# A mixer kernel's opening: chunk-wise transposes, tile-wise normalisation and the order of the first maxima

## The chip, the cores and the metric

The kernel runs on one core of a Trainium2 chip. The metric is the device time of one execution in microseconds (us), taken as the median of several runs. The engines are named as the profile names them: PE multiplies matrices (PEld loads its weights), DVE is the vector engine, ACT the scalar engine with its function tables, POOL the general engine, and SP issues the DMAs. Each engine works through its own queue in order and waits on semaphores for the others. PSUM is the memory that PE writes to; it has eight banks of 128 x 512 floats, and this kernel uses all of them.

## The reference

`x` is 2048 tokens by 512 features. It is normalised, goes through windowed attention with 32 heads of 16 features, and the result is gated by a small MLP of a second normalisation:

```python
xn = _layernorm(x)                                   # no gain, no bias
q, k, v = split(xn @ wqkv)                           # 32 heads, 16 features each
scores = q . k * 16**-0.5, kept where 0 <= query - key < 256
s = softmax(scores) @ v  -> (2048, 512) @ wo
y = _layernorm(xn)
g = silu(gelu(y @ w1 + b1) @ w2 + b2)                # 512 -> 1792 -> 512
out = x + s * g
```

Everything is float32. The kernel keeps that precision by splitting an operand into a high half and a low half (the rest that the high half leaves) and adding three products: high by high, high by low, low by high.

## The kernel before

Tokens are worked in four chunks of 512, each of four tiles of 128 tokens. For a chunk the kernel loads four tiles `xs[c]`, normalises them, transposes them on PE into banks `tr` (sixteen 128 x 128 transposes, one bank for each 128 features `kt`), and `split` writes the transposed chunk as a high half (cast on ACT) and a low half (subtraction on DVE) into `big`, called xnT in the profile. A layer norm of one tile is `bn_stats` and `bn_aggr` on DVE, an addition of eps on DVE, a power of -1/2 on POOL (`rs`), a shift on DVE and the application, an activation on ACT with scale and bias. `layernorm` has two forms. The grouped one makes the statistics of all four tiles and then one power and one shift for the four; the eager one finishes tile by tile. Before the change chunk 0 (`ln`) is eager, and chunks 1 to 3 (`ln1`, `ln2`, `ln3`) are grouped.

Heads are worked in eight groups of four. For a group n, `job_qk` multiplies a chunk with the group's q and k weights (twelve products of 128 x 512, profile name fb), and its `finish` splits the result and sends it in DMAs (`qk<-sh` for the high half, `qk<-pjr` for the low half) into the rows of a slot, from which scores are multiplied. `job_v` makes v for two blocks of 128 keys (24 products of 128 x 256, name pv) and copies them into `vt` on ACT. A slot's other rows have to hold constants: `clear_rows` writes them, ahead of the rows that the DMAs set.

Softmax needs a maximum for each query ahead of the exponentials. `max_block(n, qb)` multiplies the scores of one block of 128 queries into xy (two banks) and zo (half of two banks), merges them under a mask on DVE and reduces them on DVE, 12 blocks ahead (`LEAD`) of `prob_block`, which multiplies the scores again (stb), takes the exponential on ACT and cuts the window's edges on POOL. `pv_step` multiplies the probabilities with v into `otb`, a part of zo, and copies it out; each fourth copy is sent to `oT_d` by a DMA. `max_rows` turns four blocks' maxima into rows and sends them into the slot.

The order is written out by hand. A main loop runs over steps t from -16 to 128. Step t holds `max_block` for block t + 12, the lists `fills[t, 0]` and `fills[t, 1]` (products spread over the steps), `plan[t]` (`at`), `prob_block`, `pv_step`, `lns[t]` (layer norm steps) and `ends[t]` (`behind`). Steps -16 to -1 have no probabilities: they make projections 0 and v for all four chunks and the first twelve maxima. `groups` gives chunk c the four steps from 4c - 16, with its projection, v, the transposes of chunk c + 1, and v again. Every engine keeps this order (`Ordered`, whose line L43 all instructions carry in the profile, so that the profile is read by tile names); SP kept it only from the loop on, and the scheduler ordered its DMAs ahead of that. Ahead of the loop stands a prologue: loads, constants, chunk 0's layer norm, transposes and weight splits.

PSUM is shared out as xy (two banks), zo (two), fb0 and fb1 (one each, taken in turns by `fill_bank`) and two banks of the pool `ps_st`, which the transposes' first two banks and the v products take in turns until step 0. There the pool closes and stb takes its place.

Of the kernel before, what the change touches and what calls it, by code (L numbers as in the profile page):

```python
# [9 lines left out]
F32 = mybir.dt.float32  # L10
# [15 lines left out]
NEG = -3.0e38  # L26
LEAD = 12
EARLY = 10
FW = 128


class Ordered:
# [18 lines left out]
def mixer_kernel(ctx, tc, x, wqk, wv, wo, w1, b1, w2, b2, out):  # L51
# [27 lines left out]
        nc.sync.dma_start(t, src)  # L79
        return t  # L80

    def layernorm(ts, name, on_act, eager=False):


        n = len(ts)
        mv = small.tile([P, n, 2], F32, tag="mv", name=f"mv{name}")
        rs = small.tile([P, n], F32, tag="rs", name=f"rs{name}")
        sh = small.tile([P, n], F32, tag="shift", name=f"shift{name}")

        def each(i):  # L90

            stats(i)
            ve = small.tile([P, 1], F32, tag="ve1", name=f"ve{name}_{i}")
            nc.vector.tensor_scalar(ve, mv[:, i, 1:2], EPS, None, op0=ALU.add)
            nc.gpsimd.tensor_tensor(rs[:, i: i + 1], ve, mhalf[:, :1], op=ALU.pow)

        def shift(i):
            nc.vector.scalar_tensor_tensor(sh[:, i: i + 1], mv[:, i, 0:1], -1.0, rs[:, i: i + 1],
                                           op0=ALU.mult, op1=ALU.mult)

        def stats(i):
            st = small.tile([P, 6], F32, tag="bn", name=f"bn{name}_{i}")
# [12 lines left out]
        def apply(i):  # L115
            if on_act:
                nc.scalar.activation(ts[i], ts[i], AF.Identity, bias=sh[:, i: i + 1], scale=rs[:, i: i + 1])
            else:
                nc.vector.tensor_scalar(ts[i], ts[i], mv[:, i, 0:1], rs[:, i: i + 1],
                                        op0=ALU.subtract, op1=ALU.mult)  # L120
        if eager:
            return [(lambda i=i: each(i), lambda i=i: shift(i), lambda i=i: apply(i)) for i in range(n)]
        return [lambda i=i: stats(i) for i in range(n)] + [invert, shift_all] + [lambda i=i: apply(i) for i in range(n)]

    def run(steps):
# [43 lines left out]

    vt = vp.tile([P, NKB, 16, DH + 1], F32, name="vt")  # L170

    def clear_rows(i):

        for qk in range(2):
            nc.sync.dma_start(slots[i][3:P:4, qk].rearrange("r p (k t) -> r (p k) t", t=FW).bitcast(F32),
                              fill[:, qk].unsqueeze(1).to_broadcast([32, 4096 // FW, FW]))

    ident = const.tile([P, P], F32, name="ident")
    upper = const.tile([P, P], F32, name="upper")
    mhalf = const.tile([P, 4], F32, name="mhalf")  # L180
    negc = const.tile([P, 1], F32, name="negc")
    nc.vector.memset(negc, NEG)
    nc.vector.memset(otb, 0.0)
    mask = upper.bitcast(I32).unsqueeze(1).unsqueeze(1).to_broadcast([P, 2, 2, P])
# [60 lines left out]
    def job_qk(n, c):  # L245

        box = []
        ops = [(kt, a, b) for kt in range(KT) for a, b in PASSES]
        if not n and not c:
            ops.sort(key=lambda o: o[2])  # L250
        sl = slice(512 * c, 512 * (c + 1))

# [10 lines left out]
        def finish():  # L263
            hi = sgp.tile([P, 512], F32R, tag="sh", name=f"sh_{n}_{c}", bufs=2)
            raw = t2.tile([P, 512], F32, tag="t2", name=f"pjr_{n}_{c}")
            lo = raw.bitcast(F32R)
            nc.scalar.copy(raw, box[0])

            def high():
                nc.scalar.copy(hi, raw)  # L270
                behind(now[0], send_high)

            def send_high():
                for qk, tt in ((1, 0), (0, 0), (1, 2), (0, 1)):
                    send(hi, qk, tt)

            def low():
                (nc.gpsimd if n else nc.vector).tensor_tensor(lo, raw, hi.bitcast(F32), op=ALU.subtract)
# [205 lines left out]
    def pv_step(n, qb, also=()):  # L484
# [118 lines left out]
    for i in range(4):  # L603
        nc.sync.dma_start(xs[2][i], x[1024 + P * i: 1024 + P * (i + 1), :])
    nc.gpsimd.memset(mhalf, -0.5)
    make_identity(nc, ident)
    fill = const.tile([32, 2, FW], F32, name="fill")
    for qk in range(2):
        nc.gpsimd.memset(fill[:, qk], float(qk))
    ln = layernorm(xs[0], "A0", True, True)  # L610
# [12 lines left out]
    n, raw = raws["qk"]  # L623
    nc.gpsimd.tensor_tensor(wqs[0][:, 1], raw, wqs[0][:, 0].bitcast(F32), op=ALU.subtract)
    for j, raw in enumerate(raws["v"]):
        nc.gpsimd.tensor_tensor(wva[:, 1, 2 * j: 2 * j + 2], raw, wva[:, 0, 2 * j: 2 * j + 2].bitcast(F32),
                                op=ALU.subtract)
    nc.gpsimd.memset(vt[:, :, :, DH: DH + 1], 1.0)
    nc.gpsimd.memset(upper, 1.0)
# [7 lines left out]
    for i in range(4):  # L637
        nc.sync.dma_start(xs[3][i], x[1536 + P * i: 1536 + P * (i + 1), :])
    for i in range(4):
        nc.sync.dma_start(xn_d[i], xs[0][i])  # L640
    for i in range(4):
        at(-15, nc.sync.dma_start, xn_d[4 + i], xs[1][i])
# [75 lines left out]
    fills[16 * NQ, 0] = [(first_h, (0,))]  # L718
    at(16 * NQ, activate_first)

    ln3 = layernorm(xs[3], "A3", True)
    lns = {-16: ln1[8:] + ln2[5:6], -14: ln2[6:8], -13: ln2[8:] + ln3[0:5], -12: ln3[5:8], -11: ln3[8:]}
    def fill_in(t, half):
        now[:] = t, half
        run(delayed.pop((t, half), ()))
# [1 line left out]
            fn(*args)  # L727

    end = 16 * NQ
    nc.sync.on = True  # L730
    for t in range(-16, end + 1):
        m = t + LEAD
        if t == -5:
            open_slot(1)
            clear_rows(1)
        if 0 <= t < end:
            if t == 0:
                early.close()
                stb.append(attn.enter_context(tc.tile_pool(name="ps_s2", bufs=1, space=PSUM)).tile(
                    [P, 2, 512], F32, name="stb"))  # L740
            prob_block(t // 16, t % 16, 1)
        if 0 <= m < end:
# [12 lines left out]
        for fn, args in ends.get(t, []):  # L755
            fn(*args)
    for k in sorted(delayed):
        run(delayed[k])
    for fn, args in plan[end + 1]:
        fn(*args)  # L760
    nc.sync.on = False
    first_h(1)
# [193 lines left out]
```

## Time and profile before

| | us |
|---|---|
| median of 3 runs | 789.29 (787.99 to 789.78) |
| the profiled execution | 788.93 |
| its span in the profile | 787.2 |
| PE busy | 752.4 |
| DVE busy | 483.9 |
| ACT busy | 372.4 |
| POOL busy | 311.7 |
| first product of step 0 (stb) starts at | 73.81 |
| first PE instruction of the program starts at | 6.48 |

The profile shows one execution. A line of the timeline gives the start from the span's first instruction, the time that the group took, the engine, the line, the operation, what it wrote and read, its shape and how many there were; brackets at its end give the idle time of the engine before it, and what ended that. The page's 40 slices are 19.7 us each, with a digit for each slice in tenths of busy time.

### The profile page before, as it was taken

To read this page: it belongs to the slowest core of one execution; us is meant where nothing else is said; L and a number is where in the kernel's file an instruction comes from. 1 tells how busy PE (TensorE), PEld (TensorE's weight loads), DVE (VectorE), ACT (ScalarE), POOL (GpSimd) and SP (SyncE) were. 2 spreads that over 40 slices of the span, in tenths; PEclk is the share of its full clock that TensorE was granted. 3 is DMA by queue.
4 is the path that set the end of the run, shared out by engine and by line. 5 is a ranking of instruction groups with operands and counts; after the bars stand their busy time and mean duration, and the time that the engine had idled before them with its cause. 6 is when DMAs were issued, how large, how long until landed. Compare 5 with 4: busy or idle time off the path is not lost.

```text
span 787.2 us, 18487 instructions
## 1 busy us (share of the span) xinstructions
PE 752.4 (96%) x7420; PEld 584.8 (74%) x7420; DVE 483.9 (61%) x751; ACT 372.4 (47%) x626; POOL 311.7 (40%) x586
## 2 busy tenths in 40 slices
PE   5799999999999999999999999999999999999997
PEld 4687666666768887666666677788888888888886
DVE  5686777777777678878883558733355235532243
ACT  4643766767676666777877734321113111221111
POOL 4101665757565554767766744310112010110101
PEclk9999999999999999999999999999999999999999
DMA  8633445645446763555624282520123011210011
GB/s 272 217 75 85 109 111 130 157 109 139 110 92 213 231 217 94 131 151 138 190 88 151 81 300 82 189 87 13 54 81 116 5 41 40 82 55 13 27 54 67
DMA packets 55061, 90.46 MB, mean 115 GB/s; under 512 B 10496, under 2 KB 14848, under 8 KB 54976
## 3 DMA queue, kind: packets, MB, share of 16 engines
q1 hardware_dynamic: 54976, 89.29, 39.4%
q8 instruction: 58, 0.95, 0.5%
q14 instruction: 27, 0.22, 0.1%
HBM read 44.05 MB, written 25.95 MB: 89 GB/s over the span
## 4 chain that ended last, share of the span: by engine, by line
PE 80%; DVE 8%; ACT 5%; issue 3%; DMA 2%; POOL 1%; SPq 0%; DVEq 0%; ACTq 0%; POOLq 0%
PE acc L43 17%; PE fb L43 16%; PE h L43 15%; PE zo L43 12%; PE stb L43 7%; PE s L43 6%; PE xy L43 5%; ACT pt L43 3%; DVE xy L43 2%; DVE mt L43 2%; PE pv L43 2%; DVE xnT L43 1%; POOL pt L43 1%; PE yt L43 1%; DVE gl L43 1%
## 5 line engine op out<-in xcount | busy, mean ns | idle before, releaser
L43 POOL TENSOR_SCALAR_AFFINE_SELECT pt<-pt 128x256 f32<-128x256 f32 x480 | 195.2, 431 | 176.6 <-ACT pt L43 175.2
L43 ACT ACTIVATE pt<-stb 128x768 f32<-128x768 f32 (+1 forms) x244 | 188.6, 773 | 58.1 <-PE stb L43 48.4
L43 DVE TENSOR_REDUCE mt<-xy 128x4 f32<-128x1024 f32 (+1 forms) x128 | 152.6, 1192 | 4.4
L43 PE MATMUL acc<-w,gh 128*128 128x512 f32 x432 | 133.5, 390 | 0.3 <-DVE gh L43 0.2
L43 DVE COPY_PREDICATED xy<-upper,zo 128x512 f32<-128x512 int32 x112 | 77.6, 693 | 71.8 <-PE zo L43 69.8
L43 ACT ACTIVATE g<-h,b1s 128x512 f32<-128x512 f32 x44 | 30.3, 688 | 190.0 <-PE h L43 190.0
L43 PE MATMUL fb<-xnT,wqb 64*128 64x512 f32 (+1 forms) x696 | 117.7, 404 | 0.8 <-DVE xnT L43 0.6
L43 DVE CAST gh<-g 128x512 fp32r<-128x512 f32 x52 | 28.4, 546 | 137.6 <-PE acc L43 124.8
L43 PE MATMUL zo<-pt,vt 128*17 128x128 f32 x2880 | 103.7, 275 | 2.5 <-DVE xy L43 1.9
L43 PE MATMUL stb<-qk 64*128 64x384 f32 (+1 forms) x488 | 96.6, 392 | 7.5 <-ACT pt L43 6.0
L43 PEld LDWEIGHTS zo<-pt,vt 128*17 128x17 f32 x2880 | 67.6, 97 | 39.6 <-issue 17.9
L43 PEld LDWEIGHTS acc<-w,gh 128*128 128x128 f32 x432 | 80.8, 188 | 18.0 <-DVE gh L43 1.5
L43 PE MATMUL h<-xnT 128*128 128x512 f32 x320 | 92.0, 389 | 0.0
L43 PE MATMUL acc<-w,gl 128*128 128x512 f32 x216 | 84.6, 392 | 1.3 <-DVE gl L43 1.2
L43 PEld LDWEIGHTS stb<-qk 64*128 64x128 f32 x488 | 45.6, 183 | 52.2 <-ACT pt L43 41.2
L43 PEld LDWEIGHTS fb<-xnT,wqb 64*128 64x128 f32 (+1 forms) x696 | 65.5, 186 | 8.2 <-DVE xnT L43 0.9
L43 PEld LDWEIGHTS h<-xnT 128*128 128x128 f32 x320 | 60.1, 188 | 12.5
L43 PE MATMUL xy<-qk 64*128 64x256 f32 (+2 forms) x536 | 61.3, 302 | 4.9 <-DVE mt L43 2.3
L43 PE MATMUL h<-yh,xnT 128*128 128x512 f32 x160 | 55.7, 389 | 0.0
L43 PEld LDWEIGHTS xy<-qk 64*128 64x128 f32 x536 | 44.1, 185 | 15.6 <-DVE mt L43 6.5
L43 ACT COPY oraw<-zo 128x128 f32<-128x128 f32 x128 | 34.1, 267 | 38.3 <-PE zo L43 33.8
L43 POOL TENSOR_TENSOR or<-or,w 128x512 f32<-128x512 f32 x16 | 20.7, 1296 | 74.9 <-DMA or<-oT_d 65.6
(115 smaller groups left out, 959.9 us busy)
## 6 DMA issues: line engine op xcount, KB each, us to landing
qk<-sh SPq DMA_DIRECT2D x128, 128.0 KB
qk<-pjr SPq DMA_DIRECT2D x64, 128.0 KB
oT_d<-oraw SPq DMA_DIRECT2D x32, 256.0 KB
w_d<-in_w_dram SPq DMA_DIRECT2D x14, 512.0 KB
x<-in_x_dram SPq DMA_DIRECT2D x16, 256.0 KB
or<-oT_d SPq DMA_DIRECT2D x16, 256.0 KB
w<-rden_d SPq DMA_DIRECT2D x16, 256.0 KB
xo<-in_x_dram SPq DMA_DIRECT2D x16, 256.0 KB
```

The costliest lines, as they stand in the source:

```text
L43: r = issue(*args, **kwargs)
```

## The change

It has six parts, five of them ahead of step 0.

1. Chunk 0 is transposed tile by tile into four banks that are open at once (two of `ps_st` and the two halves of xy): as soon as a token tile is applied, its four transposes are issued. Tile 3 is applied on DVE, the others on ACT. The high halves of wv are cast on DVE, not on ACT.
2. Chunks 1 to 3 are normalised eagerly, tile by tile, and tiles 2 and 3 of chunk 1 are applied on DVE. Chunks 2 and 3 go in pairs of tiles, at the ends of steps -15, -13, -12 and -11. Before, the statistics of chunk 1 and most of chunk 2 stood in the prologue, and the rest in steps -16 to -11. Chunk 1's transposes go to both halves of xy, to zo and to one bank of `ps_st`, and half of a v product stands ahead of them.
3. `clear_rows` fills the whole slot by memsets and a copy on DVE, ACT and POOL (slot 0) or on POOL alone (slot 1); before, DMAs wrote the rows that need a constant.
4. PE gets products of constants: sixteen at the start, and three after each of the first three tiles' transposes.
5. In steps -12 to -1 `max_block` stands behind products: behind both halves of `fills` for blocks 0 to 3 and between them for blocks 4 to 11. Before, it stood ahead of them. Group 0's projections are split straight from PSUM, without the copy to SBUF, and chunk 1's projection is ordered as chunk 0's was (high halves of x first).
6. The DMA to `oT_d` is issued at the end of its step, not in the middle. SP keeps the written order from the loads of chunk 2 on, and the eight DMAs that save the normalised tiles (`xn_d`) go at the ends of steps -14 and -13.

```diff
-    def layernorm(ts, name, on_act, eager=False):
+    def layernorm(ts, name, on_act, eager=False, n_act=4):
...
-        def apply(i):
+        def apply(i, on_act=on_act):
             if on_act:
                 nc.scalar.activation(ts[i], ts[i], AF.Identity, bias=sh[:, i: i + 1], scale=rs[:, i: i + 1])
...
+        def end(i):
+
+            if i < n_act:
+                shift(i)
+            apply(i, i < n_act)
         if eager:
-            return [(lambda i=i: each(i), lambda i=i: shift(i), lambda i=i: apply(i)) for i in range(n)]
+            return [(lambda i=i: each(i), lambda i=i: end(i)) for i in range(n)]
...
-    def clear_rows(i):
-
-        for qk in range(2):
-            nc.sync.dma_start(slots[i][3:P:4, qk].rearrange("r p (k t) -> r (p k) t", t=FW).bitcast(F32),
-                              fill[:, qk].unsqueeze(1).to_broadcast([32, 4096 // FW, FW]))
+    def clear_rows(i, parts):
+
+        flat = slots[i].rearrange("p q l t -> p (q l t)")
+        ones = upper.unsqueeze(1)
+        for eng, lo, hi in parts:
+            if eng is nc.scalar:
+                eng.copy(flat[:, lo: hi].rearrange("p (k t) -> p k t", t=P), ones.to_broadcast([P, (hi - lo) // P, P]))
+            else:
+                eng.memset(flat[:, lo: hi].bitcast(F32), float(lo >= 4096))
...
+    nc.vector.memset(upper, 1.0)
+    for _ in range(16):
+        nc.tensor.matmul(fb[0][:, 0:P], upper, upper, start=True, stop=True)
+    nc.gpsimd.memset(mhalf, -0.5)
+    make_identity(nc, ident)
+    clear_rows(0, ((nc.vector, 0, 2048), (nc.scalar, 4096, 7168), (nc.gpsimd, 2048, 4096), (nc.gpsimd, 7168, 8192)))
...
             if i == 0:
-                box.append(ps_st.tile([P, 512], F32, tag="b", name=f"tr_{c}_{kt}") if kt < 2 else fill_bank())
+                box.append(xy[:, kt] if c == 1 and kt < 2 else zo[:, 0] if c == 1 and kt == 2 else
+                           ps_st.tile([P, 512], F32, tag="b", name=f"tr_{c}_{kt}") if kt < 2 or c == 1 else fill_bank())
...
-        if not n and not c:
+        if not n and c < 2:
             ops.sort(key=lambda o: o[2])
...
-            nc.scalar.copy(raw, box[0])
+            src = raw if n else box[0]
+            if n:
+                nc.scalar.copy(raw, box[0])
...
-            at(16 * n + qb + 2, nc.sync.dma_start, oT_d[n // 2, n % 2::2, :, P * (qb - 3): P * (qb + 1)], outs[0])
+            behind(16 * n + qb + 2, nc.sync.dma_start, oT_d[n // 2, n % 2::2, :, P * (qb - 3): P * (qb + 1)], outs[0])
...
+    tr0 = [ps_st.tile([P, 512], F32, tag="b", name=f"tr_0_{kt}") for kt in range(2)] + [xy[:, 0], xy[:, 1]]
+
+    def transpose0(i):
+        for kt in range(KT):
+            nc.tensor.transpose(tr0[kt][:, P * i: P * (i + 1)], xs[0][i][:, P * kt: P * (kt + 1)], ident)
+        for _ in range(3 if i < 3 else 0):
+            nc.tensor.matmul(fb[0][:, 0:P], ident, ident, start=True, stop=True)
+
+    ln = layernorm(xs[0], "A0", True, True, 3)
     for i in range(4):
         ln[i][0]()
         if i:
             ln[i - 1][1]()
-            ln[i - 1][2]()
-        if i == 3:
-            split_wqk(0)
+            transpose0(i - 1)
     ln[3][1]()
-    ln[3][2]()
-    for _, mm, k in job_x(0)[0]:
-        mm(k)
-    split_wv(0)
+    transpose0(3)
+    split_wqk(0)
     n, raw = raws["qk"]
     nc.gpsimd.tensor_tensor(wqs[0][:, 1], raw, wqs[0][:, 0].bitcast(F32), op=ALU.subtract)
     for j, raw in enumerate(raws["v"]):
+        nc.vector.tensor_copy(wva[:, 0, 2 * j: 2 * j + 2], raw)
         nc.gpsimd.tensor_tensor(wva[:, 1, 2 * j: 2 * j + 2], raw, wva[:, 0, 2 * j: 2 * j + 2].bitcast(F32),
                                 op=ALU.subtract)
+    for kt in range(KT):
+        split(big[:, 0, kt, 0:512], big[:, 1, kt, 0:512], tr0[kt])
+    ln1 = layernorm(xs[1], "A1", True, True, 2)
+    for i in range(4):
+        ln1[i][0]()
+        if 0 < i < 3:
+            ln1[i - 1][1]()
...
-    clear_rows(0)
-    ln1 = layernorm(xs[1], "A1", True)
-    run(ln1[0:4])
-    ln2 = layernorm(xs[2], "A2", True)
-    run([ln1[4], ln2[0], ln1[5], ln2[1], *ln1[6:8], ln2[2], ln2[3], ln2[4]])
...
+    for i in range(8):
+        behind(-14 + i // 4, nc.sync.dma_start, xn_d[i], xs[i // 4][i % 4])
 
     def group(c):
+        if c == 0:
+            (ops, finish), (x_ops, _) = job_v(0, 1), job_x(1)
+            return [job_qk(0, 0), job_v(0, 0), (ops[:12] + x_ops, lambda: None), (ops[12:], finish)]
...
-    ln3 = layernorm(xs[3], "A3", True)
-    lns = {-16: ln1[8:] + ln2[5:6], -14: ln2[6:8], -13: ln2[8:] + ln3[0:5], -12: ln3[5:8], -11: ln3[8:]}
+    def pair(l, a):
+        return [l[a][0], l[a + 1][0], l[a][1], l[a + 1][1]]
+
+    ln2, ln3 = (layernorm(xs[c], f"A{c}", True, True) for c in (2, 3))
+    lns = {-16: [ln1[2][1], ln1[3][1]], -15: pair(ln2, 0), -13: pair(ln2, 2), -12: pair(ln3, 0), -11: pair(ln3, 2)}
...
-            clear_rows(1)
+            clear_rows(1, ((nc.gpsimd, 0, 4096), (nc.gpsimd, 4096, 8192)))
...
-        if 0 <= m < end:
+        if t >= 0 and m < end:
             max_block(m // 16, m % 16)
         fill_in(t, 0)
         for fn, args in plan.get(t, []):
             fn(*args)
+        if 4 <= m < LEAD:
+            max_block(0, m)
         if 0 <= t < end:
             prob_block(t // 16, t % 16, 0)
         fill_in(t, 1)
+        if 0 <= m < 4:
+            max_block(0, m)
```

More of the change, by code (lines that the diff above doesn't have):

```diff
@@ L28 @@
 EARLY = 10
-FW = 128
 class Ordered:
@@ L266, in finish @@
             lo = raw.bitcast(F32R)
-            nc.scalar.copy(raw, box[0])
+            src = raw if n else box[0]
+            if n:
+                nc.scalar.copy(raw, box[0])
             def high():
-                nc.scalar.copy(hi, raw)
+                nc.scalar.copy(hi, src)
                 behind(now[0], send_high)
@@ L277, in low @@
             def low():
-                (nc.gpsimd if n else nc.vector).tensor_tensor(lo, raw, hi.bitcast(F32), op=ALU.subtract)
+                (nc.gpsimd if n else nc.vector).tensor_tensor(lo, src, hi.bitcast(F32), op=ALU.subtract)
                 behind(now[0], send_low)
@@ L602, in mixer_kernel @@
         xs[c] = [x23[:, 4 * (c - 2) + i] for i in range(4)]
[L603 to L610, printed above, removed]
+    nc.sync.on = True
+    for c in (2, 3):
+        for i in range(4):
+            nc.sync.dma_start(xs[c][i], x[512 * c + P * i: 512 * c + P * (i + 1), :])
+    tr0 = [ps_st.tile([P, 512], F32, tag="b", name=f"tr_0_{kt}") for kt in range(2)] + [xy[:, 0], xy[:, 1]]
[5 more added lines that the diff above has]
+    ln = layernorm(xs[0], "A0", True, True, 3)
     for i in range(4):
@@ L625, in mixer_kernel @@
     for j, raw in enumerate(raws["v"]):
+        nc.vector.tensor_copy(wva[:, 0, 2 * j: 2 * j + 2], raw)
         nc.gpsimd.tensor_tensor(wva[:, 1, 2 * j: 2 * j + 2], raw, wva[:, 0, 2 * j: 2 * j + 2].bitcast(F32),
                                 op=ALU.subtract)
+    for kt in range(KT):
+        split(big[:, 0, kt, 0:512], big[:, 1, kt, 0:512], tr0[kt])
+    ln1 = layernorm(xs[1], "A1", True, True, 2)
+    for i in range(4):
+        ln1[i][0]()
+        if 0 < i < 3:
+            ln1[i - 1][1]()
     nc.gpsimd.memset(vt[:, :, :, DH: DH + 1], 1.0)
-    nc.gpsimd.memset(upper, 1.0)
     nc.gpsimd.affine_select(out=upper, in_=upper, pattern=[[1, P]], compare_op=ALU.is_gt,
                             fill=0.0, base=0, channel_multiplier=-1)
-    clear_rows(0)
-    ln1 = layernorm(xs[1], "A1", True)
-    run(ln1[0:4])
-    ln2 = layernorm(xs[2], "A2", True)
-    run([ln1[4], ln2[0], ln1[5], ln2[1], *ln1[6:8], ln2[2], ln2[3], ln2[4]])
[L637 to L642, printed above, removed]
+    for i in range(8):
+        behind(-14 + i // 4, nc.sync.dma_start, xn_d[i], xs[i // 4][i % 4])
     def group(c):
+        if c == 0:
+            (ops, finish), (x_ops, _) = job_v(0, 1), job_x(1)
+            return [job_qk(0, 0), job_v(0, 0), (ops[:12] + x_ops, lambda: None), (ops[12:], finish)]
         return [job_qk(0, c), job_v(0, 2 * c), *([job_x(c + 1)] if c + 1 < NCH else []), job_v(0, 2 * c + 1)]
@@ L729, in mixer_kernel @@
     end = 16 * NQ
-    nc.sync.on = True
     for t in range(-16, end + 1):
@@ L758, in mixer_kernel @@
         run(delayed[k])
-    for fn, args in plan[end + 1]:
+    for fn, args in ends[end + 1]:
         fn(*args)
```

## The prediction

> **What bounds the kernel now.** I read the page first (busy shares, the 40 slices), then the chain, then windows and the timeline of the first 85 us, because every edit but one stands there.
>
> ```profile
> PE 752.4 (96%) x7420; PEld 584.8 (74%) x7420; DVE 483.9 (61%) x751; ACT 372.4 (47%) x626; POOL 311.7 (40%) x586
> PE   5799999999999999999999999999999999999997
> PE 80%; DVE 8%; ACT 5%; issue 3%; DMA 2%; POOL 1%; SPq 0%; DVEq 0%; ACTq 0%; POOLq 0%
> ```
>
> PE is the bound nearly everywhere; only the first two slices (39 us) show it waiting. The order on every engine behind step t = 0 is the same before and after, except for one DMA per four steps, so what the change makes of the time is how much earlier or later step 0 comes. Its first product starts at 73.81 us in the profile, and behind it the lag carries to the end.
>
> ```profile
> 20.00:25.00 5.00, 2.41 (x9) 1.56 (x10) 2.97 (x10) 4.55 (x8) 1.02 (x1) 0.84 0.95 341
> 30.00:35.00 5.00, 3.56 (x20) 2.78 (x20) 3.03 (x8) 1.97 (x4) 1.01 (x1) 1.00 0.25 69
> 35.00:40.00 5.00, 5.00 (x47) 4.66 (x46) 3.60 (x5) 4.13 (x7) 0.00 (x0) 1.00 0.49 111
> 40.00:45.00 5.00, 4.56 (x40) 4.02 (x38) 4.97 (x7) 3.04 (x7) 0.00 (x0) 1.00 0.21 46
> ```
>
> The columns after the stretch are PE, weight loads, DVE, ACT and POOL busy. Summed by windows PE idles 12.5 us up to 30 and 3.0 us from there to 75: all that can be won is before 32 us. From 40 to 45 DVE is already full (4.97 of 5).
>
> **What the edits cost.** All LayerNorm chunks now go tile by tile, as chunk 0 does already:
>
> ```profile
> 7.10 0.69 DVE L43 BATCH_NORM_STATS2 bnA<-x 128x6 f32<-128x512 f32 x1
> 8.11 0.15 DVE L43 SCALAR_TENSOR_TENSOR shiftA<-mvA,rsA 128x1 f32<-128x1 f32 x1
> 8.27 0.55 POOL L43 TENSOR_TENSOR rsA<-veA,mhalf 128x1 f32<-128x1 f32 x1 [0.53 <-DVE shiftA L43]
> 28.13 0.69 DVE L43 BATCH_NORM_STATS2 bnA<-x 128x6 f32<-128x512 f32 x1
> 28.95 0.66 DVE L43 BATCH_NORM_STATS2 bnA<-x 128x6 f32<-128x512 f32 x1
> 11.51 1.84 PE L43 MATMUL fb<-ident,x 128*128 128x128 f32 x8
> 39.76 1.04 PE L43 MATMUL fb<-ident,x 128*128 128x128 f32 x8
> ```
>
> From 7.10 one tile takes DVE 1.08 us with its small operations; in the grouped form 0.82 (28.13 to 28.95). DVE also stands still for POOL's power (0.56) ahead of the last shift. A transpose costs 0.24 us at the low clock, 0.13 at the full one.
>
> *Chunk 0.* x3 is applied on DVE at 8.86 (behind the power, 8.27 + 0.55) instead of on ACT at 9.52. The row y<-y gives 0.54, so it is done at 9.40 against 10.33, and four transposes follow, not thirteen. The constant products stand ahead of them. The trace has no plain f32 product of 128 columns; its bounds are the transpose (0.13 to 0.24) and the 128x512 product (3.03 for 12, 0.25). I take 0.25, since PE gets its first work at 1.1: then three products and four transposes take 1.27 a tile, and the first bank is complete at about 11 (9.95 to 15). DVE meanwhile makes both high halves of wv, moved to it from ACT, while POOL subtracts. What that does shows late in the trace:
>
> ```profile
> 468.31 0.43 DVE L43 CAST gh<-g 128x512 fp32r<-128x512 f32 x1 [5.54 <-PE acc L43]
> 473.75 1.55 DVE L43 CAST gh<-g 128x512 fp32r<-128x512 f32 x1 [0.16 <-PE acc L43]
> 473.71 2.74 POOL L43 TENSOR_TENSOR wos<-wos 128x512 fp32r<-128x512 f32 x2
> ```
>
> The same cast takes 0.43 alone and 1.55 beside POOL's subtraction. So the copies end at 11.4 (0.43 + 1.55 from 9.4), not 10.3. Then come the four splits: casts of 0.58, subtractions of 0.69. In the built order the fourth cast waits for the third subtraction, because both read the one tile xy. That gives 11.75, 12.4, 13.1, 13.8, a cast to 14.4 and the last subtraction to 15.1. Before, it ended at 14.69: nothing is won (bounds 13.9, copies and products free, and 18.5, products at the low clock).
>
> *Chunk 1.* Four tiles at 1.08 from 15.1, power, and the apply on DVE (0.54): x3 of the chunk is ready at 20.55 (before 23.5). PE does fb and both v products meanwhile and transposes the first bank by 20.9. The second bank is xy's other half, and in the built order its first transpose waits for the DVE subtraction of the first half. That waits for its ACT cast, and this stands behind the applies of two x2 tiles. Two halves of one tile do wait for each other in this kernel, as the view of waits shows; otb is a part of zo that the masked copy does not touch:
>
> ```profile
> PE zo L43 <- DVE xy L43: 1.9, 6, 0.5
> ```
>
> DVE: pjr 0.69 to 21.25, two x2 tiles to 23.4, power and shift to 24.1; ACT: apply 0.81 to 24.95, cast to 25.55; DVE: subtraction to 26.3. PE stands 5.4 us. Then twelve transposes at 0.24 (29.2), the second half of v (1.9, 31.1), fb 2.99 (34.1) and the first maxima product 0.44: 34.55. Before, the same work ended at 34.79. Again nothing.
>
> The transposes are priced at 0.24 because the trace shows what such a gap does: behind the idle time from 20 to 23 us the granted clock is 0.50 from 24 to 26 and 1.00 from 27.
>
> *Chunk 2.* Before, DVE had all of x2's and x3's statistics done by 31.4. Now it has two x2 tiles and four x3 tiles left, between the maxima. DVE in its order: x2 tiles to 33.55; maxima 0 (0.75 + 0.69, from 34.6) to 36.05; two x3 tiles with power 38.95; pjr 39.65; maxima 1 (0.76 + 1.23) 41.65; two x3 tiles 44.55. ACT must apply both (0.81 each, to 45.5) before its first cast of chunk 2 (46.1), and DVE's subtraction ends at 46.8. PE: v 37.65, maxima 38.0, first bank 38.5; the next bank waits for the copy of vt, which stands on ACT behind two x3 applies (40.55); transposes 42.1, maxima 42.7. The next v product waits for a bank until 46.8, and runs to 49.95; maxima 3 waits for DVE (three subtractions, 0.69 + 1.23) to 50.75 and ends at 51.35. Before, that work was done at 44.72: 6.6 us late. This is the term that decides: idle 2.05 + 4.15 + 0.8. If the gap of 4.15 halves the clock as that at 20 to 23 did, for some 3 us, v costs 1.5 more, of which 0.8 hides in the wait for maxima 3: +0.7, kept for the range.
>
> The Trainium skill (TensorE: Matmul & The Clock Gate, Part 1) says that the clock halves after an idle window of about 3.4 us and returns after as long a busy one. By that rule the v product would start slow and the sum would be some 0.9 higher; the trace has one such spell, and agrees.
>
> *Chunk 3 to step 0.* DVE's backlog is gone. PE waits 0.55 for maxima 3, then runs as before; the small waits before (0.52 at 59.4) are partly hidden by putting maxima behind products. My sum reaches the end of maxima 9 and fb at 70.1, against 63.79: 6.3 late. Step 0 is at 80.1.
>
> *The rest.* Projection 0 is split straight from PSUM: an ACT copy of 0.56 less for each chunk, and the bank is held until DVE's subtraction (39.65), ahead of the transposes that want it. The four DMAs that set the rows go; their cover was idle queue time. On SP they and eight xn_d writes no longer stand ahead of the first rows, which land by about 26 (needed at 34.1): the 1.7 us that PE waited for them at 31.4 is in the sum. Engines set slot 0 instead: 2048 on DVE before x lands at 3.41, 3072 on ACT (0.81 for 768, so under 3.3 us) before 5.6, and 3072 on POOL. POOL's rows bound that: ident (0.204 for 128, 0.098 for one, 0.83 ns an element) ends it at 4.2 and costs nothing, vt (0.576 for 256, 1.87 ns) at 7.2 and then delays the first power of 4.59, +1.9. I take ident, a plain fill like this. Slot 1 takes POOL twice 3.4 us from 61.7, free until step 0. The output DMA moved behind the step passes three or four row DMAs on SP (0.55 each); PE's only row wait there is 0.7: 0 to -0.7, I take 0.
>
> **Sum.** +0.4 (chunk 0), -0.6 (chunk 1), +6.8 (chunk 2), -0.3: +6.3 us on the profiled execution's 788.93 (0.36 under the median): 795.2.
>
> **Rivals.** *DVE's backlog fits its slack (faster).* The order on DVE might bind less than I make it. If chunk 2's waits (2.05, 4.15, 0.8) and the 0.55 all vanish, 795.2 - 7.55 = 787.6; with free copies 786.7. It decides where the tiles between maxima 0 and the v product of 46.8 cost 4.7 us less than my 10.7 (then within 0.2%) and 7.9 less (faster). For it: PE had no wait there before; against: the order is fixed, and 40 to 45 shows DVE full without them.
>
> *POOL's long fills hold DVE (slower still).* The fills of slot 1 run 61.7 to 68.5 and the rows of the maxima are cast on DVE at 66.85.
>
> ```profile
> L43 DVE CAST mh<-mt x32: 160/198/378, 45.7 to 422.3; 128x16 fp32r<-128x16 f32 x32
> ```
>
> If that cast waits as gh's did, +1.7; cold products, POOL's slower rate or the slow v product add 0.7 to 3.4: 797 to 800. Against it: at most 0.38 beside selects of 0.43, with POOL half busy. The Trainium skill (SBUF — State Buffer, "SBUF: two separate sides") has VectorE and GpSimd share a port pair that one of them holds for a whole instruction. By it the fill would be waited out (796.9); gh's row agrees, mh's hardly does.
>
> *Half the waits.* If the second bank or the vt copy comes earlier than I make it, 790 to 792.
>
> **How the numbers follow.** Forecast (793 to 797) 0.55, slower still 0.20, half 0.10, backlog hidden 0.15. The range, 790 to 800, leaves out the hidden backlog and little above. About 0.2% (1.6 us) is what a measurement can tell: faster 0.12, within 0.07 (from the last two cases), slower 0.81.
>
> **What will show it.** A PE gap of 4 to 6 us near 21 to 26 ended by DVE xnT with transposes of 0.24 behind it; DVE without gaps from 30 to 50; a PE gap near 43 to 47; the first stb product near 80. I am wrong if stb comes before 75, or if PE's gaps end with DMA or POOL.

## The result, and the profile after

The changed kernel takes 812.9 us (median of 6 runs, 805.7 to 816.7) against 789.4 for the kernel before: ratio 1.029 (95% 1.024 to 1.033), 23.5 us slower. The forecast was 795.2, with a range that ended at 800. The sign was right and the size was short by some 18 us.

The profiled execution took 812.72 us, its span is 810.7. From the page of the changed kernel, the busy shares, the slices of PE and the chain by engine:

```profile
PE 765.0 (94%) x7470; PEld 596.9 (74%) x7470; DVE 494.0 (61%) x773; ACT 369.7 (46%) x618; POOL 325.5 (40%) x596
PE   8678999999999999997899999899999999999997
PE 72%; DMA 8%; DVE 7%; issue 4%; ACT 4%; POOL 2%; SPq 1%; ACTq 0%; DVEq 0%; POOLq 0%
```

Three things are new. PE has more idle time in slices 3 and 4 (41 to 81 us), which were full. It also has some at slices 19, 20 and 26, far behind step 0, where the forecast expected no change at all. And DMA holds 8% of the chain; before it held 2%.

The span splits at three marks: the first stb product (step 0), the last copy of an attention output (oraw<-zo), and the end.

| | before | after | longer by |
|---|---|---|---|
| start to first stb | 73.81 | 84.05 | 10.2 |
| first stb to last oraw copy | 379.72 | 391.43 | 11.7 |
| last oraw copy to end | 333.7 | 335.2 | 1.5 |

The first row is what the forecast was about. The second row it put at zero. The third is about as large as the same stretch varies between the runs below (333.0 to 335.3), and nothing is built on it.

**Ahead of step 0.** The timeline of PE in the changed kernel, its longer waits up to step 0 (start, duration; in brackets the idle time ahead and what ended it):

```profile
25.96 1.11 PE L42 MATMUL xy<-ident,x 128*128 128x128 f32 x4 [5.14 <-DVE xnT L42]
...
40.53 0.66 PE L42 MATMUL tr<-ident,x 128*128 128x128 f32 x4 [1.65 <-ACT vt L42]
...
46.61 5.49 PE L42 MATMUL pv<-wva,xnT 128*128 128x256 f32 x24 [3.95 <-DVE xnT L42]
52.03 0.67 PE L42 MATMUL xy<-qk 64*128 64x256 f32 x4
...
73.32 0.50 PE L42 MATMUL xy<-qk 64*128 64x256 f32 x4 [1.98 <-DVE mt L42]
...
84.05 0.44 PE L42 MATMUL stb<-qk 64*128 64x384 f32 x2 [0.21 <-ACT vt L42]
```

The first three waits are those of the forecast (5.4, 2.05 and 4.15) at the places it named. Behind the third, the v product takes 5.49 us where 24 such products took 3.13. The stretches of five microseconds show why, in the column of the granted clock (third from the end):

```profile
40.00:45.00 5.00, 2.13 (x20) 1.82 (x20) 3.75 (x10) 1.68 (x4) 1.10 (x2) 1.00 0.23 52
45.00:50.00 5.00, 3.39 (x16) 3.39 (x17) 4.10 (x6) 2.82 (x6) 0.00 (x0) 0.56 0.01 3
50.00:55.00 5.00, 4.54 (x26) 3.63 (x25) 2.83 (x5) 0.59 (x1) 0.00 (x0) 0.76 0.00 0
```

The wait of 1.98 at 73.32 is the rival of the long fills. The timeline of POOL and DVE in the changed kernel has the fill of slot 1 and the cast of the maxima beside it:

```profile
63.95 6.98 POOL L42 MEMSET qk<- 128x4096 f32 x2 [19.63 <-PE fb L42]
68.50 2.46 DVE L42 CAST mh<-mt 128x16 fp32r<-128x16 f32 x1
```

The cast (0.20 in the median before) ends at 70.96, when the second memset ends (70.93).

**Behind step 0.** Waits from 85 to 480 us (total, times, longest), of the kernel before and then of the changed one. First what SP and PE waited for before:

```profile
SPq L43 <- DMA mT_d<-mT: 6.0, 5, 2.6
PE stb L43 <- ACT pt L43: 6.0, 15, 1.0
```

```profile
SPq L42 <- DMA mT_d<-mT: 36.3, 11, 6.4
ACT xnT L42 <- DMA xnT<-w_d: 7.1, 2, 4.5
ACT oraw L42 <- DMA oT_d<-oraw: 6.2, 5, 2.1
PE stb L42 <- ACT pt L42: 12.9, 18, 4.4
```

SP now stands 36.3 us until the 16 KB of the maxima's rows have landed (mT_d), ahead of the DMA that reads them back. ACT, which waited 0.5 us for DMAs before, now waits 13.3: for weights (xnT<-w_d) and for output stores to land (oT_d<-oraw), as a copy into oraw needs the buffer that an earlier store reads. ACT works in order, so the exponentials behind (pt) come late for stb. The place of the longest of these waits, as SP issues it in the changed kernel:

```profile
377.62 0.52 SPq L42 DMA_DIRECT2D oT_d<-oraw  x1
378.18 1.05 SPq L42 DMA_DIRECT2D xnT<-w_d  x2
379.33 1.59 SPq L42 DMA_DIRECT2D qk<-pjr  x2
381.02 0.55 SPq L42 DMA_DIRECT2D mT_d<-mT  x1
388.00 0.55 SPq L42 DMA_DIRECT2D qk<-mT_d  x1
388.65 0.52 SPq L42 DMA_DIRECT2D oT_d<-oraw  x1
```

and at the same place before:

```profile
360.61 0.91 SPq L43 DMA_DIRECT2D xnT<-w_d  x2
361.62 1.80 SPq L43 DMA_DIRECT2D qk<-pjr  x2
363.53 0.55 SPq L43 DMA_DIRECT2D mT_d<-mT  x1
365.65 0.54 SPq L43 DMA_DIRECT2D oT_d<-oraw  x1
366.29 0.53 SPq L43 DMA_DIRECT2D qk<-mT_d  x1
```

Before, the store's 256 KB followed the 16 KB, and went out while SP waited for them anyway: 2.8 us from the write's issue to the read's. Now the store goes out behind the read, right ahead of two weight transfers of 256 KB each and two row DMAs of 128 KB each; the next 16 KB come behind all 1 MB, and 7.0 us pass from the write's issue to the read's. But PE does not wait for SP here: the weights that ACT waits for were issued ahead of SP's wait, at 378.18, right behind the store. The timeline of ACT, in the changed kernel and then the same cast before:

```profile
386.35 0.62 ACT L42 CAST xnT<-xnT 128x512 fp32r<-128x512 f32 x1 [4.54 <-DMA xnT<-w_d]
```

```profile
366.25 0.61 ACT L43 CAST xnT<-xnT 128x512 fp32r<-128x512 f32 x1
```

The weights are there some 8 us after their issue; before, they were there when ACT came, 5.6 us after it. The timeline of PE in the changed kernel, where ACT's wait arrives:

```profile
387.73 0.69 PE L42 MATMUL stb<-qk 64*128 64x384 f32 x2 [4.45 <-ACT pt L42]
```

PE goes on at 387.73, ahead of SP (388.00).

### The profile page after: what moved, and what is told of

It is laid out like the page before. It is cut to its first block, busy times and chain, and to the rows that moved or that the text cites. A ratio compares the mean times of both kernels' runs of the same rounds, so it can differ in the third digit from the quotient of the medians.

```text
span 810.7 us, 18609 instructions
## 1 busy us (share of the span) xinstructions
PE 765.0 (94%) x7470; PEld 596.9 (74%) x7470; DVE 494.0 (61%) x773; ACT 369.7 (46%) x618; POOL 325.5 (40%) x596
## 4 chain that ended last, share of the span: by engine, by line
PE 72%; DMA 8%; DVE 7%; issue 4%; ACT 4%; POOL 2%; SPq 1%; ACTq 0%; DVEq 0%; POOLq 0%
PE acc L42 15%; PE h L42 14%; PE fb L42 14%; PE zo L42 10%; PE stb L42 6%; PE s L42 5%; DMA oT_d<-oraw 4%; PE xy L42 4%; ACT pt L42 3%; PE pv L42 2%; DMA xnT<-w_d 2%; DVE mt L42 2%; DVE xy L42 2%; SPq L42 1%; DVE xnT L42 1%
## 5 line engine op out<-in xcount | busy, mean ns | idle before, releaser
L42 PEld LDWEIGHTS h<-xnT 128*128 128x128 f32 x320 | 60.1, 188 | 12.5
L42 PEld LDWEIGHTS xy<-qk 64*128 64x128 f32 x536 | 45.0, 188 | 14.5 <-DVE mt L42 7.8
L42 ACT COPY oraw<-zo 128x128 f32<-128x128 f32 x128 | 34.2, 267 | 43.0 <-PE zo L42 33.8
```

What stands on the lines that cost most here:

```text
L42: r = issue(*args, **kwargs)
```

## The experiments

Each was timed in at least four executions beside the kernel before, whose median was 789.2 to 789.5 every time. "Stretch" is the time from the first stb product to the last oraw copy in the profiled execution.

| run | median us | ratio (95%) | first stb | stretch |
|---|---|---|---|---|
| changed kernel | 812.9 | 1.029 (1.024 to 1.033) | 84.05 | 391.4 |
| e1 store back in mid-step | 798.2 | 1.011 (1.010 to 1.013) | 83.08 | 379.0 |
| e2 store moved in the kernel before | 795.7 | 1.008 (1.006 to 1.010) | 73.60 | 386.8 |
| e9 store behind its step, one step earlier | 798.1 | 1.011 (1.009 to 1.012) | 83.71 | 379.4 |
| e3 e1 + slot 1 filled in eight pieces | 797.1 | 1.010 (1.008 to 1.012) | 80.91 | 379.0 |
| e4 e1 + second bank in fb[0] | 794.7 | 1.006 (1.005 to 1.008) | 81.16 | 378.9 |
| e5 e1 + chunks 2 and 3 grouped | 791.3 | 1.002 (1.001 to 1.004) | 75.99 | 379.8 |
| e6 e1 + e3 + e4 + e5 | 788.2 | 0.998 (0.996 to 0.999) | 72.71 | 379.5 |
| e8 e6 without constant products | 787.1 | 0.997 (0.995 to 0.999) | 72.75 | 379.4 |
| e11 e8, x2's statistics later | 788.5 | 1.000 (0.998 to 1.002) | 72.63 | 380.2 |
| e12 e11, two of x3's later too | 790.1 | 1.001 (0.999 to 1.003) | 75.55 | 379.6 |
| e7 maxima behind products in the kernel before | 788.0 | 0.998 (0.996 to 0.999) | 73.34 | 379.0 |
| e10 e6 with the store moved | 799.5 | 1.013 (1.011 to 1.015) | 72.01 | 389.4 |

**The store (e1, e2, e9).** Only the store's place differs:

```diff
-            behind(16 * n + qb + 2, nc.sync.dma_start, oT_d[n // 2, n % 2::2, :, P * (qb - 3): P * (qb + 1)], outs[0])
+            at(16 * n + qb + 2, nc.sync.dma_start, oT_d[n // 2, n % 2::2, :, P * (qb - 3): P * (qb + 1)], outs[0])
```

> The changed kernel with one part undone: the DMA that stores four finished output blocks (oT_d<-oraw) is issued in the middle of its step again, ahead of the read of the maxima's rows, and not behind the step. In the changed kernel the stretch from the first stb product (84.05) to the last oraw copy (475.48) is 391.4 us, before it is 379.7 (73.81 to 453.53). Theory A: this 11.7 us comes from the moved DMA alone: 256 KB now lie in the queues with the weight transfers ahead of the 16 KB of the maxima's rows, SP stands until those have landed, and all behind it is late. Then the stretch falls back to 380, the first stb product stays at 84, and the time is 800 to 802. Theory B: the 11.7 us come from the prologue's new order (the steps meet the weight transfers 10 us later, other buffers are free at other times): the stretch stays at 390 or more and the time at 811 to 814.

> The kernel before with this part alone: the store of the output blocks moved behind its step, nothing else. Theory A (the moved DMA makes the loss behind step 0): the first stb product stays at 73.8, the stretch from it to the last oraw copy grows from 379.7 by 8 to 13 us, and the time is 797 to 803. Theory B (the loss comes from the prologue): within 1 us of the kernel before, 788 to 790.

e1 takes 14.7 us off, its stretch is back at 379.0, and the first stb product hardly moves: theory A as to the cause. Which wait carries the loss is taken up below. e2 loses 6.4 us with the line moved the other way in the kernel before. That is theory A's sign at half its size, and below the 8 that were expected.

```diff
-            behind(16 * n + qb + 2, nc.sync.dma_start, oT_d[n // 2, n % 2::2, :, P * (qb - 3): P * (qb + 1)], outs[0])
+            behind(16 * n + qb + 1, nc.sync.dma_start, oT_d[n // 2, n % 2::2, :, P * (qb - 3): P * (qb + 1)], outs[0])
```

> The changed kernel with the output store still behind its step, but one step earlier: SP then issues it right behind the write of the maxima's rows (mT_d<-mT) and not, as in the changed kernel, behind the read of them and right ahead of the weight transfers. Theory A: what costs is that the 256 KB of the store lie next to the weights and ahead of the following 16 KB of maxima's rows. Then this place is as good as the middle of the step: the stretch from the first stb to the last oraw copy is 379 to 382 (391.4 in the changed kernel) and the time 797 to 801. Theory B: any store behind a step loses, since ACT's copy into oraw waits for it later: the stretch stays above 386 and the time above 805.

e9 has the store behind a step too, but right behind the write of the rows, and it loses nothing: the time of e1. The same view of SP's waits, for e2 and then for e9:

```profile
SPq L43 <- DMA mT_d<-mT: 34.5, 11, 5.8
```

```profile
SPq L42 <- DMA mT_d<-mT: 6.4, 5, 2.6
```

So it is not the end of a step that costs. SP issues its DMAs in e9 in nearly the order of e1 (10 of 496 places differ), and what the store stands ahead of in that order decides. That its bytes count, and not only its place, is argued from the sizes (256 KB and 16 KB): no run changes the store's size.

**The fill (e3), on top of e1.**

```diff
-            clear_rows(1, ((nc.gpsimd, 0, 4096), (nc.gpsimd, 4096, 8192)))
+            clear_rows(1, [(nc.gpsimd, 1024 * k, 1024 * k + 1024) for k in range(8)])
```

> As the changed kernel with the output store in the middle of its step, and the fill of slot 1 cut on POOL from two memsets of 4096 columns into eight of 1024; POOL's work stays the same. In the changed kernel the cast mh takes 2.46 us beside such a memset (0.17 elsewhere) and the maxima's product waits 1.98 for it. If DVE is kept out for one whole memset, the cast takes at most 0.85 + 0.2 here, the wait falls below 0.6, and the time is 1.4 to 2.0 us under that of the run with the store alone put back. If it is something else that holds the cast (POOL's traffic as such), the time stays the same within 0.5 us.

```profile
62.37 7.24 POOL L42 MEMSET qk<- 128x1024 f32 x8 [19.16 <-PE fb L42]
66.92 0.90 DVE L42 CAST mh<-mt 128x16 fp32r<-128x16 f32 x1
```

POOL's work is the same (7.24 for 6.98). The cast takes 0.90 and ends at 67.82; six of the eight pieces (0.905 each) end at 67.80. The cast is kept out for one whole instruction of POOL, so short ones cost little. Not every operation of DVE is: beside the long memset a masked copy and a reduction from PSUM (66.52 and 67.24 in the changed kernel) take 0.69 and 1.23, as they do elsewhere. PE's wait falls from 1.98 to 0.41 and step 0 comes 2.2 us earlier in the profile; the medians differ by 1.1, less than expected, and as the intervals overlap, the times alone don't show the gain. The Trainium skill (SBUF — State Buffer, "SBUF: two separate sides") says the same of the port pair that GpSimd shares with VectorE operations of certain forms: one holds it for a whole instruction and the other blocks. The two casts agree with it.

**The second bank (e4), on top of e1.**

```diff
-                box.append(xy[:, kt] if c == 1 and kt < 2 else zo[:, 0] if c == 1 and kt == 2 else
+                box.append((xy[:, 0], fb[0], zo[:, 0])[kt] if c == 1 and kt < 3 else
```

> As the changed kernel with the output store in the middle of its step, and the second bank of the second chunk's transposes in fb[0], which is free there, in place of xy's second half. My prediction took the 5.4 us for which PE stands at 21 to 26 for a wait of one half of the tile xy on the other's split. If so, the 16 transposes follow each other without the gap, PE's next wait is for the splits ahead of projection 0, the first maxima product comes 3 to 5 us before 34.4, and step 0 1 to 4 us earlier than in the run with the store alone put back. Rival: what DVE has to do before the first maxima (statistics of four x2 tiles) decides, and the gap only moves on: maxima 1 and 2 then wait for DVE, step 0 is earlier by less than 1 us.

The timeline of PE in e4:

```profile
26.09 5.49 PE L42 MATMUL fb<-xnT,wqb 128*128 128x512 f32 x12 [2.99 <-DVE xnT L42]
...
44.00 5.41 PE L42 MATMUL pv<-wva,xnT 128*128 128x256 f32 x24 [3.94 <-DVE xnT L42]
```

The sixteen transposes follow each other; PE then waits 2.99 for the splits. The first maxima product comes at 31.51 (33.88 in e1), 2.9 us before 34.4 and a little less than the 3 to 5 expected, as the projection behind the gap runs at half clock (5.49 us, 2.91 in e1). Step 0 gains 1.9 us, the median time 3.5 (the two profiled executions differ by 2.3). The wait of 3.94 ahead of the third v product is untouched (3.95 in the changed kernel): it is a loss of its own.

**The backlog (e5), on top of e1.** Chunks 2 and 3 grouped, all statistics ahead of the first maxima:

```diff
-    ln2, ln3 = (layernorm(xs[c], f"A{c}", True, True) for c in (2, 3))
-    lns = {-16: [ln1[2][1], ln1[3][1]], -15: pair(ln2, 0), -13: pair(ln2, 2), -12: pair(ln3, 0), -11: pair(ln3, 2)}
+    ln2, ln3 = (layernorm(xs[c], f"A{c}", True) for c in (2, 3))
+    lns = {-16: [ln1[2][1], ln1[3][1]] + ln2[0:6], -14: ln2[6:8], -13: ln2[8:] + ln3[0:5], -12: ln3[5:8], -11: ln3[8:]}
```

> As the changed kernel with the output store in the middle of its step (798.2), and the LayerNorm of chunks 2 and 3 in the grouped form of the kernel before: four statistics, one power, one shift, and all of a chunk's statistics ahead of the first maxima; chunk 1 stays by tiles. Theory A (my prediction's term of 6.8 us): what loses in chunk 2 is that four x3 tiles stand between the maxima on DVE, so the waits of PE for ACT's vt (1.65), for DVE ahead of the third v product (3.95, with the half clock behind it) and for maxima 3 go; step 0 comes 4 to 6 us earlier (77 to 79 against 83.1), the time is 792 to 794. The statistics of x2 now stand ahead of chunk 1's splits, so the wait for xy's second half stays at 4 to 6 us. Theory B: the backlog only moves ahead, chunk 1's splits are later by what chunk 2 wins: 796.5 to 798.5.

Step 0 comes 7.1 us earlier (75.99), the time falls by 6.9. The waits for vt and ahead of the third v product (1.65 and 3.95 in the changed kernel) are gone, and with them the low clock there. The window in which the changed kernel had 0.56, in e5:

```profile
45.00:50.00 5.00, 4.53 (x29) 3.60 (x29) 4.45 (x8) 0.59 (x1) 0.00 (x0) 1.00 0.02 3
```

The first wait stays (5.57 for xy's second half, as expected). Theory A, with a little more won than it expected. The run changes the form and the place of the statistics at once. That the place counts, e12 below shows (grouped too, but with two statistics behind the first maxima); what the form is worth alone is not measured.

**All four, and the constant products (e6, e8).** e8 drops the sixteen products at the start and the three behind each token tile.

> All four edits to the changed kernel together: output store in the middle of its step, slot 1 filled in eight pieces, chunk 1's second bank in fb[0], LayerNorm of chunks 2 and 3 grouped and early. If the terms add (14.7, 1.1, 3.5, and 4 to 6 for the grouped form), the time is 787 to 790, step 0 at 73 to 76: what is left of the change (chunk 0 by token tile, constant products, rows set by engines, maxima behind products) is then worth within 2 us of nothing, as my prediction summed it. If the bank and the backlog are one and the same loss, the terms overlap and the time stays at 791 to 793.

> The run with all four edits, without the 16 products of a constant with itself ahead and the three behind each token tile's transposes (they write to a bank that nothing reads). If they keep TensorE's clock up, the transposes of chunk 0 take 0.24 us each again (0.11 to 0.13 with them) and the first projection is slower: step 0 comes 0.5 to 2 us later than with them. If they only fill time in which PE waits anyway, the time is the same within 0.5 us.

The terms overlap little: e6 takes 788.2, 10.0 us less than e1, where the three edits alone took 1.1, 3.5 and 6.9 (11.5). What is left of the change is worth 1.1 us against the kernel before. In e8 the transposes are slow again (0.69 us for two, 0.38 with the products), as the first theory has it, and yet step 0 is at the same place (72.75 against 72.71): the slow transposes fit into the time between two tiles. e8 is the fastest kernel of the case, 0.3% under the kernel before; its interval overlaps e6's, so the products are not shown to cost anything either.

**Where e6's remaining wait goes (e11, e12).** In e6 and e8 PE still waits 3.42 us for chunk 1's splits.

```diff
-    lns = {-16: [ln1[2][1], ln1[3][1]] + ln2[0:6], -14: ln2[6:8], -13: ln2[8:] + ln3[0:5], -12: ln3[5:8], -11: ln3[8:]}
+    lns = {-16: [ln1[2][1], ln1[3][1]], -14: ln2[0:8], -13: ln2[8:] + ln3[0:5], -12: ln3[5:8], -11: ln3[8:]}
```

> The run with all four edits without the constant products (787.1), and x2's statistics moved on DVE behind chunk 1's four splits. There PE stood 3.42 us for the splits ahead of projection 0's second chunk, which then ran at half clock (5.49 us in place of 2.99). If that wait is DVE's, it falls under 1 us, the projection is back at 3.0, the first maxima product comes 4 to 5 us earlier, and step 0 2 to 5 us earlier: 782 to 785. If DVE's sum of work up to the third chunk's splits is the bound, the wait only moves to the maxima or the splits of chunk 2: 786 to 788.

> As the run with x2's statistics behind chunk 1's splits, and two of x3's four statistics behind the first maxima too. If DVE has slack there, the first maxima's reduction comes 1.6 us earlier and the time is 0 to 1.5 us under that run. If the pattern of the changed kernel returns (statistics between the maxima, then late splits of chunk 2), it is 1 to 3 us above it.

The timeline of PE in e11, and its clock from 35 to 40:

```profile
33.05 0.80 PE L42 MATMUL xy<-qk 64*128 64x256 f32 x4 [3.77 <-DVE mt L42]
```

```profile
35.00:40.00 5.00, 4.86 (x26) 4.41 (x27) 3.89 (x6) 4.05 (x8) 0.00 (x0) 0.53 0.38 88
```

The wait for the splits is gone and the first maxima product comes 6.2 us earlier (25.78), but PE then waits 3.77 for the maxima, and step 0 is where it was (72.63). The product behind that wait is still 2.4 us earlier than in e8 (33.05 against 35.45). The low clock that follows takes this back: the product of maxima 3 starts at 42.34, against 42.46. So moving DVE's work moved the wait, and the slow clock took what was won. That DVE's sum of work is the bound is not shown: behind the slow transposes DVE itself waits 1.11 us for ACT's cast. e12 pushes two of x3's statistics behind the first maxima, and the changed kernel's pattern returns (3.87 us for vt, step 0 2.9 us later).

**Maxima behind products (e7), alone in the kernel before.**

> The kernel before with this part alone: the first head group's maxima (ahead of step 0) stand behind the first or second half of a step's products in place of ahead of them. My prediction gave it almost nothing (0 to 0.5 us won, through small waits that are covered). Then the time is 788.5 to 789.5. Rival: the maxima go through DVE to the rows that step 0 needs, so putting them later makes step 0 later by up to half a step's products, 1 to 2 us slower: 790 to 791.5.

Step 0 comes 0.5 us earlier and the time is 1.2 us lower (0.12% to 0.37%): a small gain, a little above what was expected, and about as much as all that is left of the change in e6.

**The size of the store's loss (e10 and the repeats).** The same line cost 14.7 us in the changed kernel and 6.4 in the kernel before. e10 moves it in e6.

> The run with all four edits (788.2), but with the store of the output blocks behind its step as in the changed kernel. The same move cost 14.7 us in the changed kernel and 6.4 on the kernel before, and the order of work behind step 0 is the same in both. If the prologue sets the size (step 0 late, so everything else meets the transfers differently), the cost here is that on the kernel before, 5 to 8 us: 793 to 797. If something else of the change sets it (the fills, or the prologue's transfers), it is 12 to 16: 800 to 805.

It costs 11.3, between the two ranges, with step 0 as early as before. The three were then measured again on one chip.

> The changed kernel itself, on one chip with the two others that have the store behind its step. If the program sets what the moved store costs, it is 811 to 814 again, 10 or more above the kernel before with the move alone after the prologue's 8.9 are taken off. If the chip sets it, the three costs come out alike: 804 to 807 where the move alone costs 6, 808 to 811 where it costs 11.

> The kernel before with the store's move alone, on the same chip. If the program sets the cost: 795 to 797, as before. If the chip sets it: within 2 us of the cost that the two others show here.

> The run with the prologue repaired and the store behind its step, on the same chip. If the program sets the cost: 798 to 801 (11 over 788.2). If the chip sets it: the kernel before plus the cost of the move alone here, less 1.

812.3 (806.8 to 812.9), 796.7 (795.9 to 797.6) and 799.4 (794.8 to 802.4): nearly the medians of before. The changed kernel stays clear of the other two, so the program sets its cost and not the chip. The third overlaps the second here; that those two differ rests on e10 and e2 (1.011 to 1.015 against 1.006 to 1.010), measured on two chips. The places are much the same too: between the two kernels with and without the move, the lag jumps near 166, 190, 284, 352 and 368 us of the kernel before, and at the same steps of the changed one. The largest difference lies in one of them, the weight transfers near 380, where ACT waits 4.54 us in the changed kernel and 1.85 in e2. What in the rest of the change makes that one longer is open. The changed kernel's own executions differ by 11 us, e1's by 1.3.

What goes with the loss is the sum of ACT's waits for weights and stores, and not SP's wait for the 16 KB. From 85 to 480 us, in us, with the growth of the stretch against the same kernel without the move (e1, the kernel before, e6), where ACT has no such waits:

| run | stretch grows by | ACT waits | SP waits |
|---|---|---|---|
| changed kernel | 12.5 | 13.3 | 36.3 |
| changed kernel, repeated | 13.5 | 12.6 | 34.4 |
| e10 | 9.8 | 10.1 | 30.8 |
| e10, repeated | 5.2 | 6.0 | 33.4 |
| e2 | 7.1 | 8.9 | 34.5 |
| e2, repeated | 9.0 | 9.3 | 33.8 |

## Why the prediction failed

**The failed step is the last one, "The rest":** "The output DMA moved behind the step passes three or four row DMAs on SP (0.55 each); PE's only row wait there is 0.7: 0 to -0.7, I take 0." It counted the store as one issue of 0.5 us that moves past others, and asked who waits for those others. It left out that the store is 256 KB ahead of weights in a shared queue, and that ACT waits in its own order for these weights and for the store's landing (13.3 us, none in e1). PE's rows, the only thing that it asked about, are not what PE waits for. Measured: +14.7 (the changed kernel against e1). With it falls the sentence that what the change makes of the time "is how much earlier or later step 0 comes".

**The prologue's mechanisms held, one by one.**

| step of the forecast | forecast | measured |
|---|---|---|
| chunk 0's last split ends | 15.1 | 14.63 |
| wait for xy's second half | 5.4, transposes at 0.24 | 5.14, transposes at 0.21 |
| first maxima product starts | 34.1 | 34.36 |
| wait for the copy of vt | 2.05 | 1.65 |
| wait ahead of the third v product | 4.15 | 3.95 |
| maxima 3 start | 50.75 | 52.03 |
| step 0 | 80.1 | 84.05 |

The term of chunk 2, 6.8 us, is what e5 gives back (6.9 in time, 7.1 in step 0). The rival "DVE's backlog fits its slack" is out. One of the prediction's signs failed, "DVE without gaps from 30 to 50": DVE is busy 14.5 of these 20 us. It waits 1.88 for PE, 0.60 at a time for POOL's power and 1.35 for ACT's cast ahead of the late splits. The prediction's own times had drawn one of these gaps (33.55 to 34.6). So the wait of 3.95 stands behind a chain through DVE, POOL and ACT, and not behind a full DVE. The first row of the table is near by luck: the two casts of wv, priced at 0.43 + 1.55, took 0.76 together, and DVE then waited 1.21 for ACT's first cast.

**Two terms were kept for the range that belonged in the sum.** The v product at half clock was +0.7 at most; it cost 1.3 (maxima 3 at 52.03 instead of 50.75), and the sum itself had drawn a gap of 4.15 us ahead of it, like the one behind which the transposes were rightly priced slow. The cast held by POOL's fill was a rival at 1.7 with two chances in ten; the wait is 1.98 and e3 shows it. The row taken against it (mh at most 0.38) came from selects of 0.43 us, and says nothing of a memset of 3.5. With these two, step 0 comes out at 83.4; 0.6 us stays unassigned (step 0 is at 83.1 to 84.05 in four profiles of this prologue). Without the store the time is 798.2, inside the forecast's range and in the rival "slower still" (797 to 800).

**Also confirmed:** the constant products and chunk 0 by token tile win nothing (e8, and 14.63 against 14.69); the rows that PE waited 1.67 us for before (at 31.44) are waited for no longer, and the first maxima are no earlier than the chain ahead of them allows (34.36).

## What to carry to other kernels

A DMA that is moved counts with its bytes and its neighbours, not with its issue: ask which transfers it now stands ahead of, and which engine waits in its order for one of them or for the buffer that the moved one frees. Here a large store was free where the queue waited for a small round trip anyway, and costly ahead of weights. Taking work out of one wait's way can set up the next (e11), and a gap that is drawn in the sum should be priced with the slow clock behind it.

## What was not expected of the hardware

A wait far shorter than the half clock it brings can already start it. In e2, PE waits 1.74 us, and 1.4 us after the wait's end (374.56, by the 0.78 below) the granted clock falls to 0.50, for 3.4 us (it is 0.52 from 377 to 378); the timeline of PE and the windows of e2:

```profile
373.20 0.44 PE L43 MATMUL stb<-qk 64*128 64x384 f32 x2 [1.74 <-ACT pt L43]
```

```profile
374.00:375.00 1.00, 1.00 (x10) 0.62 (x8) 0.79 (x2) 0.60 (x2) 0.38 (x2) 0.78 0.03 10
375.00:376.00 1.00, 1.00 (x18) 0.49 (x16) 1.00 (x1) 1.00 (x2) 1.00 (x3) 0.50 0.43 49
```

The wait of 2.99 in e4 is followed by half clock for 5.49 us, while those of 1.65 and 1.98 in the changed kernel are followed by products at full speed. In e1 the same wait of 1.65 is followed by half clock. The transposes behind it on PE, in the changed kernel and then in e1:

```profile
41.02 1.04 PE L42 MATMUL fb<-ident,x 128*128 128x128 f32 x8
```

```profile
40.55 1.88 PE L42 MATMUL fb<-ident,x 128*128 128x128 f32 x8
```

So the length of the wait alone does not decide; what does is open. The Trainium skill (TensorE: Matmul & The Clock Gate, Part 1) gives an idle window of about 3.4 us. Waits of 1.65, 1.74 and 2.99 with the low clock behind them disagree with it taken as a length that a wait must reach, and the runs decide. The prediction took the one spell in the kernel before as in agreement; the longest single wait of PE ahead of that spell, from 20 to 23 us, is 1.50. So PE's loss from a late transfer is more than the wait: in the changed kernel six products fb take 1.59 us behind the wait of 4.45, and 0.91 ahead of it.
